# A new hand-written engine order for a cross-attention and PReLU kernel, with weight loads issued at other places and wider filler products

## The chip, the cores and the metric

The kernel runs on one core of one Trainium2 chip. The metric is device time in microseconds (us) of one execution, the median over runs. The engines are TensorE (PE in the profile; its weight loads are PEld), VectorE (DVE), ScalarE (ACT), GpSimd (POOL) and SyncE (SP). The first four compute; SP here only issues DMA transfers, and POOL and ACT issue some too.

## The reference

There are 8 batches of 8 heads. `x` is 512 tokens of 64 numbers per head, `state` 32 states of 64 numbers per head. Tokens read states and states read tokens, and all 544 rows of a batch then go through a two-layer network of widths 512, 2048, 512 with a PReLU between.

```python
scores = scale * np.matmul(x, state.transpose(0, 1, 3, 2))
a = softmax(scores)                       # over 32 states
xread = np.matmul(a, state)
scores2 = scale * np.matmul(state, x.transpose(0, 1, 3, 2))
a2 = softmax(scores2)                     # over 512 tokens
sread = np.matmul(a2, x)
x = np.concatenate([xread, sread], axis=2)   # heads side by side: (8 * 544, 512)
h = x @ w_in
g = np.maximum(h, 0.0) + alpha * np.minimum(h, 0.0)
out = g @ w_out
```

## The kernel before

**What is computed, and how.** For the tokens, `xread @ w_in` is not formed from `xread`: the states of a batch are multiplied into `w_in` first (`m`, line 445), and the softmax weights are then multiplied into that (`h`, lines 478 and 499). So the first product of the network has the states as its depth. For the rows that belong to states, all 8 batches are collected in `XS` and go through `w_in` at the end (line 487). The weights are kept in SBUF: `w_in` in four parts by columns of the hidden layer (`wi.0` to `wi.3`), `w_out` in four parts by its rows (`wo.0` to `wo.3`). A part is 512 KB as float16. Hidden columns are numbered in 16 pieces of 128 (`jc`): `wi.f` and `wo.f` both hold pieces 4f to 4f+3.

**The order.** The program is run from the string `ORDER` (lines 17 to 102): a list of some thousand steps. Each step is a short name, a dot, and arguments; the loop at line 607 calls the function of that name (table at line 593). Every engine works through its own steps in the order of the list, and waits at a step until what that step needs is there. Semaphores are put in from the data dependencies. The names, by engine:

- POOL, loads: `lx0.g` (half g of the first batch's x, line 179), `lx.b` (x of batch b, line 162), `lst` (all states but the first batch's, line 192), `wi.f` (line 198), `wo.i` (line 204). `id` makes the identity matrix that transposes use.
- TensorE: `Z.k.n` (n filler products of zeros of 128 columns into PSUM bank k, lines 213 to 217), `stt` and `str` (states transposed), `xt.b.j.g.k` (a quarter of x of batch b transposed, line 281), `sc.b` or `sc.b.half` (the scores, line 295), `m.b.f` (states times part f of w_in, line 445), `F.b.jc.k` (the first product of piece jc, two instructions, line 478; of the rows of states if b is 8, four instructions, line 487), `f.b.jc.g` (one half of such a product, line 499), `S.b.q.j` (second product: token quarter q, pieces 2j and 2j+1, line 530), `rd.b` (states reading tokens, line 420), `R` (second product of the rows of states, line 578), `L` (second product of the last quarter in three column pieces, line 550).
- DVE and ACT, `.a` for ACT, `.v` for DVE, `.p` for POOL: `xo` (transposed x out of PSUM), `sto`, `sro` (transposed states out), `mo.b.f.e.g` (a half of m out, line 467), `N.b.jc` (ACT: the negative part of h, line 510), `G.b.jc` (DVE: PReLU from h and N, line 518), `O.b.q` (an output quarter out of PSUM and to DRAM, lines 568 and 571), `rdo` (line 431), `stc` (the first states cast, line 238), `oma` (DVE: one less alpha from a loaded alpha, four transposes and one operation, lines 251 and 252).
- The softmax over states of batch b, a chain over three engines: `sb` (DVE: scores transposed in blocks, line 328 or 330), `smax` (DVE, line 336), `ssh` (POOL: subtract, line 342), `sexp` (ACT, line 348), `ssum` (DVE: sum and reciprocal, lines 352 and 353), `snorm` (POOL: multiply, line 356), `wb` (DVE: transposed back, line 364). Batch 0 does it in two halves, `.0` and `.1`.
- The softmax over tokens: `tm` (DVE, line 376), `te` (ACT, line 387), `tsum` (DVE, line 397), `tn` (POOL, line 401), `tt` (SP: transposed by DMA, line 405). `xd.b` (SP) transposes x of a later batch by DMA (line 273).

**PSUM.** Six banks are named 0 to 5 by the number at the end of a step, and one two-bank tile ("two") is shared by the scores and by those `m` that name no banks. A step that takes a bank waits until the reader of the bank's last content is through: for a piece of h that is its `G`, for an output its `O`, for an m its `mo`, for the scores `sb`, `tm` and `te`.

**Around the change.** Before the zero fillers there is a memset of a tile of zeros (line 211). Fillers stand at the head, where TensorE has nothing else to do. The head's real work is: transposes of the first states and of x of batch 0, its scores, m of part 0 for batches 0 to 3, transposes of x of batch 1, and then the first products f and F of batch 0, for which each part of w_in has to have landed.

```python
    zero = consts.tile([128, 128], F16)
    nc.vector.memset(zero, 0.0)

    def zeros(k, n):
        t = single(k, f"z_{len(zs)}", [128, 128], F32)
        zs.append(t)
        for _ in range(n):
            nc.tensor.matmul(t, zero, zero, start=True, stop=True)
```

Of the kernel before, what the change touches and what calls it, by code (L numbers as in the profile page):

```python
# [28 lines left out]
S.0.0.2 N.0.9 G.0.6 S.0.1.2 smax.1 te.1.1 te.1.0 F.0.11.4 G.0.9 ssh.p.1 F.0.8.3 N.0.8 N.0.11 S.0.0.3  # L29
S.0.1.3 m.0.3 G.0.8 F.0.10.0 mo.0.3.a.0 N.0.10 sexp.1 S.0.2.3 mo.0.3.v.1 xd.2 G.0.11 G.0.10  # L30
S.0.3.0.3 m.1.3 S.0.3.1 mo.1.3.a.0 F.0.14.4 S.0.2.4 F.0.13.0 N.0.14 tt.0 ssum.1 S.0.0.4 S.0.1.4
S.0.0.5 S.0.3.2 G.0.14 F.0.12.4 N.0.13 G.0.13 F.0.15.0 snorm.p.1 N.0.12 N.0.15 mo.1.3.a.1 wb.1
S.0.3.3 S.0.1.5 S.0.3.4 G.0.12 S.0.2.5 G.0.15 S.0.3.5 F.1.2.4 S.0.2.6 N.1.2 F.1.0.0 tsum.1 S.0.2.7
N.1.0 S.0.1.6 S.0.1.7 G.1.2 O.0.2.a sc.2 m.2.1.4.5 S.0.0.6 O.0.1.a F.1.7.2 mo.2.1.a.0 mo.2.1.a.1
G.1.0 F.1.1.0 tm.2 sb.2 F.1.3.4 N.1.7 S.0.0.7 S.0.3.6 N.1.1 G.1.1 N.1.3 tn.1.0 O.0.0.a te.2.0
F.1.5.5 S.0.3.7 N.1.5 G.1.3 F.1.9.0 S.1.1.0.1 G.1.7 F.1.4.4 smax.2 O.0.3.a S.1.1.1 tn.1.1 G.1.5
rd.0.2 te.2.1 N.1.9 G.1.9 m.2.3 F.1.6.3 N.1.4 rdo.0.a F.1.12.5 N.1.6 lx.3 G.1.4 F.1.13.2 N.1.12
F.1.8.0 G.1.6 G.1.12 S.1.2.0.4 N.1.13 G.1.13 ssh.p.2 N.1.8 S.1.1.2 F.1.11.3 G.1.8 F.1.10.5 N.1.11
S.1.2.1 N.1.10 G.1.11 G.1.10 S.1.2.2 sexp.2 S.1.1.3 ssum.2 F.1.14.2 F.1.15.0 snorm.p.2 mo.2.3.a.0
S.1.1.4 mo.2.3.a.1 S.1.1.5 m.3.2 m.4.2.3.5 N.1.14 tt.1 tsum.2 N.1.15 G.1.14 mo.3.2.a.1 S.1.1.6  # L40
S.1.2.3 S.1.2.4 mo.3.2.a.0 mo.4.2.a.0 G.1.15 mo.4.2.a.1 S.1.2.5 S.1.1.7 xd.3 O.1.1.a m.3.1.2.0
m.2.2.3.5 sc.3 wb.2 tn.2.1 S.1.2.6 S.1.2.7 mo.3.1.a.1 F.2.15.1 S.1.0.0.0 mo.2.2.a.0 mo.3.1.a.0
O.1.2.a lx.4 mo.2.2.a.1 sb.3 N.2.15 S.1.0.1 tm.3 F.2.13.3 N.2.13 G.2.15 S.1.0.2 F.2.4.2 tn.2.0
F.2.2.4 G.2.13 smax.3 N.2.4 F.2.9.5 F.2.0.1 N.2.9 S.1.0.3 S.1.0.4 G.2.9 S.1.0.5 N.2.2 N.2.0 te.3.0
F.2.12.3 S.1.0.6 N.2.12 G.2.2 G.2.4 G.2.0 xd.4 F.2.7.5 G.2.12 S.1.3.0.4 ssh.p.3 sexp.3 N.2.7 ssum.3
S.1.0.7 te.3.1 F.2.3.2 S.1.3.1 F.2.1.1 N.2.3 S.1.3.2 N.2.1 F.2.8.3 G.2.3 S.1.3.3 G.2.1 S.1.3.4
S.1.3.5 N.2.8 S.1.3.6 G.2.7 F.2.6.2 O.1.0.a N.2.6 m.3.3.1.0 G.2.8 sc.4 rd.1.5 snorm.p.3 F.2.5.3
G.2.6 mo.3.3.a.0 F.2.14.1 rdo.1.a wb.3 N.2.5 tsum.3 S.2.1.0.2 F.2.11.5 mo.3.3.a.1 G.2.5 S.1.3.7
N.2.14 F.2.10.0 F.3.4.3 G.2.14 N.2.11 S.2.1.1 F.3.1.1 lx.5 O.1.3.v N.3.4 S.2.1.2 N.2.10 G.2.11 tt.2
S.2.0.0.4 S.2.1.3 S.2.0.1 G.2.10 F.3.14.5 F.3.9.0 S.2.1.4 tn.3.1 N.3.1 N.3.9 G.3.1 S.2.1.5 S.2.0.2  # L50
G.3.4 tn.3.0 N.3.14 tm.4 F.3.3.1 F.3.8.3 G.3.14 N.3.8 G.3.9 S.2.1.6 S.2.1.7 S.2.0.3 S.2.3.0.5 N.3.3
xd.5 O.2.1.a tt.3 sb.4 G.3.8 smax.4 F.3.6.0 F.3.2.2 te.4.0 S.2.3.1 S.2.3.2 N.3.6 N.3.2 F.3.13.3
S.2.0.4 te.4.1 ssh.p.4 N.3.13 G.3.3 G.3.6 S.2.0.5 F.3.7.1 G.3.2 S.2.0.6 N.3.7 S.2.0.7 sexp.4 G.3.13
G.3.7 S.2.3.3 S.2.3.4 S.2.3.5 m.6.0 O.2.0.v m.5.1.0.2 mo.6.0.a.1 mo.5.1.a.1 rd.3.3 mo.6.0.v.0
rdo.3.a mo.5.1.v.0 rd.2.1 m.4.1.4.2 ssum.4 sc.5 m.4.3.0.3 rdo.2.a S.2.3.6 mo.4.1.a.1 mo.4.1.a.0 tm.5
tsum.4 snorm.p.4 F.3.5.1 mo.4.3.a.0 mo.4.3.a.1 F.3.0.2 F.3.10.4 N.3.0 S.2.3.7 O.2.3.a S.2.2.0.0
S.2.2.1 F.3.11.3 G.3.0 wb.4 S.2.2.2 S.3.3.0.5 F.3.15.2 S.3.3.1 N.3.5 lx.6 G.3.5 te.5.0 te.5.1 N.3.10
N.3.15 S.2.2.3 F.3.12.1 S.2.2.4 N.3.11 S.3.3.2 lx.7 N.3.12 G.3.10 G.3.15 F.4.6.4 N.4.6 tn.4.0
F.4.5.2 G.3.11 F.4.3.3 N.4.5 S.2.2.5 G.3.12 G.4.5 S.3.3.3 F.4.4.1 S.3.3.4 F.4.7.2 N.4.4 S.3.3.5
S.2.2.6 N.4.3 sb.5 N.4.7 S.3.3.6 S.2.2.7 G.4.4 G.4.7 S.3.3.7 F.4.1.1 F.4.0.2 xd.6 O.2.2.a S.3.1.0.0  # L60
O.3.3.a S.3.1.1 F.4.9.5 N.4.1 smax.5 G.4.6 N.4.0 S.3.0.0.4 tn.4.1 S.3.0.1 G.4.1 G.4.0 F.4.8.1
S.3.1.2 tsum.5 N.4.9 ssh.p.5 G.4.3 sexp.5 N.4.8 G.4.9 F.4.11.2 F.4.2.3 N.4.2 S.3.0.2 ssum.5 S.3.0.3
S.3.0.4 tt.4 N.4.11 S.3.1.3 G.4.8 S.3.1.4 S.3.1.5 G.4.2 S.3.1.6 snorm.p.5 m.5.0.5.1 G.4.11 sc.6
m.5.3.3.2 xd.7 wb.5 mo.5.0.a.1 sb.6 S.3.1.7 mo.5.3.a.0 mo.5.0.a.0 F.4.13.1 N.4.13 S.3.0.5 mo.5.3.a.1
S.3.2.0.3 tm.6 S.3.0.6 te.6.0 F.4.10.5 F.5.3.2 smax.6 S.3.2.1 N.4.10 N.5.3 S.3.2.2 S.3.2.3 S.3.0.7
S.3.2.4 S.3.2.5 S.3.2.6 ssh.p.6 G.4.13 O.3.1.a tn.5.0 F.4.14.1 te.6.1 O.3.0.v S.3.2.7 G.4.10 G.5.3
N.4.14 F.4.12.0 G.4.14 O.3.2.a sexp.6 tn.5.1 S.4.1.0.4 m.6.3 m.7.2.5.2 m.5.2.3.1 mo.6.3.v.0 S.4.1.1
mo.5.2.v.0 mo.7.2.a.0 S.4.1.2 mo.5.2.a.1 F.5.15.5 mo.6.3.v.1 mo.7.2.a.1 tt.5 S.4.1.3 N.5.15 G.5.15
F.4.15.3 F.5.12.1 S.4.1.4 F.5.5.2 N.4.12 F.5.13.5 S.4.1.5 N.5.12 N.4.15 G.4.12 tsum.6 G.4.15
S.4.0.0.0 S.4.1.6 S.4.1.7 N.5.5 S.4.0.1 S.4.2.0.3 O.4.1.v G.5.5 S.4.0.2 F.5.10.4 N.5.13 F.5.1.2  # L70
S.4.2.1 G.5.12 F.5.0.1 N.5.10 S.4.0.3 S.4.2.2 S.4.0.4 G.5.13 tn.6.1 N.5.0 G.5.10 N.5.1 G.5.1
m.6.1.5.4 m.7.0 mo.6.1.a.1 mo.6.1.a.0 S.4.0.5 mo.7.0.v.0 S.4.0.6 F.5.2.2 N.5.2 S.4.0.7 mo.7.0.v.1
G.5.0 O.4.0.a rd.4.4 rd.5.5 G.5.2 m.7.3.1.0 rdo.4.a m.6.2.2.4 sc.7 rdo.5.a ssum.6 mo.7.3.a.0
mo.6.2.a.0 snorm.p.6 tn.6.0 S.4.3.0.5 S.4.3.1 mo.7.3.v.1 F.5.11.1 S.4.3.2 sb.7 S.4.3.3 N.5.11 G.5.11
F.5.6.2 F.5.9.0 S.4.2.3 S.4.2.4 F.5.7.1 S.4.3.4 mo.6.2.a.1 F.5.8.4 smax.7 S.4.3.5 S.4.3.6 wb.6
S.4.3.7 S.4.2.5 N.5.9 N.5.8 N.5.7 G.5.9 O.4.3.a G.5.8 F.5.4.0 N.5.4 tt.6 S.5.0.0.4 S.5.2.0.5 S.4.2.6
G.5.7 G.5.4 F.5.14.1 S.5.2.1 tm.7 S.5.0.1 N.5.6 S.4.2.7 F.6.3.0 N.5.14 G.5.6 S.5.2.2 S.5.0.2 te.7.1
F.6.15.2 N.6.3 G.6.3 S.5.2.3 N.6.15 S.5.2.4 S.5.0.3 G.6.15 ssh.p.7 S.5.2.5 F.6.7.0 S.5.1.0.2 N.6.7
S.5.0.4 G.5.14 O.4.2.v S.5.1.1 F.6.6.1 G.6.7 F.6.8.3 te.7.0 S.5.1.2 N.6.6 S.5.1.3 sexp.7 F.6.1.0
tsum.7 N.6.8 N.6.1 G.6.6 S.5.2.6 F.6.0.1 S.5.0.5 tn.7.1 tn.7.0 S.5.0.6 G.6.8 S.5.2.7 F.6.10.3 tt.7  # L80
N.6.0 S.5.1.4 G.6.1 S.5.1.5 S.5.1.6 S.5.1.7 F.6.14.0 N.6.10 O.5.1.a ssum.7 G.6.10 S.5.0.7 F.6.5.3
snorm.p.7 F.6.2.2 N.6.14 N.6.5 G.6.0 S.5.3.0.1 O.5.0.v G.6.14 m.7.1 G.6.5 rd.7.4 rd.6.0 rdo.7.v
N.6.2 O.5.2.a F.6.13.3 S.5.3.1 mo.7.1.v.0 rdo.6.a S.5.3.2 S.5.3.3 mo.7.1.v.1 F.6.9.5 F.8.4.4 N.6.9
G.6.2 S.5.3.4 wb.7 F.6.12.0 G.6.9 F.6.4.2 N.6.13 N.6.12 S.5.3.5 G.6.12 N.6.4 S.5.3.6 S.5.3.7
S.6.0.0.5 S.6.0.1 N.8.4 F.6.11.0 G.6.13 G.6.4 F.8.10.3 N.6.11 S.6.0.2 N.8.10 O.5.3.v G.8.4 S.6.1.0.2
F.7.0.1 S.6.0.3 F.7.7.4 N.7.0 S.6.1.1 G.6.11 S.6.0.4 N.7.7 S.6.0.5 G.7.0 S.6.1.2 F.8.14.0 S.6.1.3
S.6.1.4 G.8.10 S.6.0.6 N.8.14 F.7.3.1 S.6.0.7 G.7.7 S.6.1.5 F.8.3.3 F.7.6.4 G.8.14 N.7.3 F.8.2.0
O.6.0.v G.7.3 F.7.2.5 F.8.9.1 S.6.1.6 N.8.3 G.8.3 S.6.2.0.3 N.8.2 N.7.2 S.6.2.1 G.8.2 S.6.2.2 N.7.6
# [17 lines left out]
def kernel(  # L106
# [106 lines left out]
    def zeros(k, n):  # L213
        t = single(k, f"z_{len(zs)}", [128, 128], F32)
        zs.append(t)
        for _ in range(n):
            nc.tensor.matmul(t, zero, zero, start=True, stop=True)  # L217
# [422 lines left out]
```

## Time and profile before

| | |
|---|---|
| median of 3 runs | 218.81 us (218.28 to 219.42) |
| the profiled execution's own time | 219.05 us |
| its span, first to last instruction | 217.3 us |
| granted TensorE clock over the span | 1.00 |
| TensorE busy 0 to 5, 5 to 10, 10 to 15 us | 3.73, 4.53, 3.47 us |
| TensorE, DVE, ACT busy 20 to 25 us | 4.92, 5.00, 4.70 us |
| TensorE, DVE, ACT busy 100 to 120 us | 20.00, 18.62, 13.74 us |
| second product (L530), 496 instructions | 125.3 us busy, 379 ns each |
| first product (L478), 250 instructions | 68.3 us busy, 379 ns each |
| fillers (L217), 82 instructions | 7.5 us busy, 262 ns each |
| PReLU (L518), 128 full instructions | 89.9 us busy, 738 ns each |
| negative part (L510), 144 instructions | 76.9 us busy, 577 ns each |

Instructions of one engine overlap: a product of 512 columns lasts 379 ns, but the next starts 0.216 us after it. So a busy engine's rate is read from the starts of instructions that follow each other without a wait, not from the mean duration. Of the execution's 219.05 us, 1.75 lie around the span.

### The profile page before, as it was taken

What the parts mean: (1) busy time and instruction counts of PE and PEld (TensorE: products, weight loads), DVE (VectorE), ACT (ScalarE), POOL (GpSimd) and SP (SyncE); (2) the same over time, 40 slices, a digit from 0 to 9 for tenths busy, and PEclk for the clock granted to TensorE, in tenths of its full rate; (3) what the DMA queues carried; (4) which work ended last, traced back from release to release, by engine and by line L of the source; (5) the groups of instructions that cost most, each with busy time, mean ns of one, the idle gap of its engine ahead of it and who ended that gap; (6) DMA issues with size and microseconds to landing.
All of it is one profiled execution on the core that took longest, in us unless ns stands there. A gap on an engine that the chain in (4) does not pass through costs nothing.

```text
span 217.3 us, 4317 instructions
## 1 busy us (share of the span) xinstructions
PE 210.2 (97%) x1698; PEld 104.0 (48%) x1698; DVE 166.5 (77%) x255; ACT 137.6 (63%) x271; POOL 71.1 (33%) x58
## 2 busy tenths in 40 slices
...
GB/s 88 173 198 208 195 195 176 139 203 136 54 139 147 53 227 111 51 99 193 236 52 100 97 50 51 0 100 48 50 149 9 40 51 48 48 37 11 51 97 145
DMA packets 39716, 23.12 MB, mean 106 GB/s; under 512 B 22144, under 2 KB 35984, under 8 KB 39696
## 3 DMA queue, kind: packets, MB, share of 16 engines
...
q8 instruction: 13, 0.21, 0.4%
q14 instruction: 7, 0.06, 0.1%
...
## 4 chain that ended last, share of the span: by engine, by line
PE 87%; DMA 8%; POOL 2%; issue 1%; DVE 1%; ACT 0%; POOLq 0%
PE o L530 48%; PE h L478 24%; DMA w_in_sb<-in_moe_w_in_dram 5%; PE m_ps L445 4%; PE h L487 3%; PE o L578 3%; DMA xT<-xg 3%; PE o L550 2%; PE sr_ps L420 2%; PE sc L295 1%; DVE m L467 1%; POOL xg L179 1%; POOL xg L162 0%; PE h L499 0%; POOL w_in_sb L198 0%
## 5 line engine op out<-in xcount | busy, mean ns | idle before, releaser
L530 PE MATMUL o<-w_out_sb,gt 128*128 128x512 f16 x496 | 125.3, 379 | 0.0
L510 ACT ACTIVATE neg<-h 128x512 f32<-128x512 f32 (+1 forms) x144 | 76.9, 577 | 46.9 <-PE h L478 37.4
L518 DVE SCALAR_TENSOR_TENSOR gt<-neg,oma_sb,h 128x512 f16<-128x512 f32 x128 | 89.9, 738 | 15.8 <-ACT neg L510 14.7
L530 PEld LDWEIGHTS <-gt 128*128 128x128 f16 x496 | 47.3, 98 | 55.4 <-issue 3.4
L478 PE MATMUL h<-aT,m 128*128 128x512 f16 x250 | 68.3, 379 | 0.0
L478 PEld LDWEIGHTS <-m 128*128 128x128 f16 x250 | 24.1, 98 | 28.4 <-issue 0.6
L401 POOL TENSOR_SCALAR e<-e,r 128x512 f16<-128x512 f16 x16 | 25.0, 1568 | 21.1 <-DVE r L397 17.5
L467 ACT CAST m<-m_ps 128x512 f16<-128x512 f32 x50 | 27.0, 603 | 5.0 <-PE m_ps L445 4.6
L356 POOL TENSOR_TENSOR an<-ts,r 128x1024 f16<-128x1024 f32 (+1 forms) x9 | 15.5, 1720 | 33.9 <-DVE r L353 14.8
L342 POOL TENSOR_TENSOR ts<-ts,mx 128x1024 f32<-128x1024 f32 (+1 forms) x9 | 15.5, 1721 | 28.5 <-DVE mx L336 28.5
L568 ACT COPY osb<-o 128x512 f32<-128x512 f32 x22 | 12.9, 591 | 14.9 <-PE o L530 14.9
L445 PE MATMUL m_ps<-w_in_sb,stT 64*32 64x512 f16 x256 | 11.3, 383 | 0.9 <-DMA w_in_sb<-in_moe_w_in_dram 0.7
L387 ACT ACTIVATE e<-sc,nb 128x512 f16<-128x512 f32 x16 | 11.1, 700 | 1.1 <-DVE nb L379 1.1
L364 DVE STREAM_TRANSPOSE aT<-an 128x1024 f16<-128x1024 f16 (+1 forms) x9 | 10.1, 1120 | 1.8 <-POOL an L356 1.8
L518 DVE SCALAR_TENSOR_TENSOR gs<-neg,oma_sb,h 128x256 f16<-128x256 f32 x16 | 7.5, 478 | 4.5 <-ACT neg L510 4.5
L467 DVE CAST m<-m_ps 128x512 f16<-128x512 f32 x14 | 9.1, 679 | 2.1 <-ACT m L467 1.6
L352 DVE TENSOR_REDUCE r<-ts 128x32 f32<-128x1024 f32 (+1 forms) x9 | 9.9, 1095 | 0.0
L336 DVE TENSOR_REDUCE mx<-ts 128x32 f32<-128x1024 f32 (+1 forms) x9 | 9.8, 1092 | 0.0
L376 DVE TENSOR_REDUCE nb<-sc 128x2 f32<-128x1024 f32 x8 | 9.6, 1204 | 0.3 <-PE sc L295 0.3
L487 PE MATMUL h<-XS,w_in_sb 128*128 128x256 f16 x64 | 9.4, 273 | 0.0
L588 DVE COPY osr<-o 128x512 f32<-128x512 f32 x1 | 0.7, 691 | 11.3 <-PE o L578 11.3
L217 PE MATMUL z<-zero 128*128 128x128 f16 x82 | 7.5, 262 | 1.4 <-DVE zero L211 1.1
...
## 6 DMA issues: line engine op xcount, KB each, us to landing
...
```

Of the source, the lines that this page charges most:

```text
L342: engine(e).tensor_tensor(ts, ts, over_blocks(cols(live["mx", b], j, S // N)), ALU.subtract)
L356: engine(e).tensor_tensor(blocks(cols(live["an", b], j, S)), blocks(cols(live["ts", b], j, S)), over_blocks(cols(live["r1", b], j, S // N) ...
L387: nc.scalar.activation(live["e2", b][:, g, :, :], live["sc", b][:, :, :, g, :].rearrange("p r j s -> p (r j) s"), EXP, bias=live["nb", b][ ...
L401: nc.gpsimd.tensor_scalar_mul(e2, e2, live["r2", b][:, g : g + 1])
L445: nc.tensor.matmul(t[N * k : N * (k + 1), :], st_head(b, h)[64 * r : 64 * r + 64, :], w_in_sb[64 * r : 64 * r + 64, c, 512 * f : 512 * (f ...
L467: copier(e)(m_tile(b)[:, f, g, :], live["mp", b, f][g])
L478: nc.tensor.matmul(h.rearrange("p (r j s) -> p r j s", r=2, j=2), ms[b][:, f, g, 128 * j : 128 * (j + 1)], weights(b, g), start=(g == 0), ...
L487: nc.tensor.matmul(h, w_in_sb[:, c, 128 * jc : 128 * (jc + 1)], XS[:, c].rearrange("p q n b -> p (q n b)"), start=(c == 0), stop=(c == n_c ...
L510: nc.scalar.activation(neg, h, RELU, bias=0.0, scale=-1.0)
L518: nc.vector.scalar_tensor_tensor(gt, negs.pop((b, jc)), oma_sb[:, jc : jc + 1], h, ALU.mult, ALU.add)
L530: nc.tensor.matmul(outs[b, q], gts[b, jc][:, 128 * q : 128 * (q + 1)], w_out_sb[:, jc, :], start=(jc == 0), stop=(jc == n_jc - 1),)
L568: copier(e)(osb, t)
```

## The change

Four things are changed.

1. The tile of zeros is 512 columns wide, and `Z.k.n` now makes n times 128 columns in as few instructions as possible, up to 512 columns each. The fillers' numbers are changed in the list.
2. In the head, the loads are issued earlier in POOL's sequence: wo.0 and wi.2 directly behind wi.1, ahead of the first batch's `ssh`; wo.2, lx.2 and wo.3 directly behind both `tn` of batch 0. The sequence of the loads among themselves stays as it is.
3. Steps of the head change place or engine: `oma` comes behind the first two copies of x, `sto` goes from ACT to DVE, the x copies and the copies of m change engines and order, `m.0.1` uses the two-bank tile.
4. The list behind that, up to the sixth batch, is another sequence of the same steps, with other banks, and with some copies on another engine (`snorm` of batch 4 and `ssh` of batch 7 on DVE, for instance). In the last part, from the middle of the first products of batch 7 on, the sequence is the same but for the numbers of the banks.

```diff
 ORDER = """
-stc lx0.0 lx0.1 oma id Z.1.20 stt.0 Z.2.18 xt.0.0.0.1 sto.a xt.0.1.0.2 xo.0.0.0.v lst xo.0.1.0.v
-Z.0.6 sc.0.0 xt.0.1.1.3 xt.0.0.1.4 sb.0.0 xo.0.0.1.v smax.0.0 xo.0.1.1.a str.0.5 sc.0.1 str.1.0 wi.0
-sro.0.a lx.1 wi.1 ssh.p.0.0 sb.0.1 Z.1.3 sc.0 Z.5.7 m.0.0.1.2 sro.1.a sexp.0.0 smax.0.1 m.3.0.3.4
-ssh.p.0.1 tm.0 mo.0.0.a.1 sexp.0.1 ssum.0.0 m.1.0.5.0 ssum.0.1 te.0.1 te.0.0 mo.1.0.v.1 wo.0
-mo.1.0.a.0 snorm.p.0.0 mo.3.0.a.1 Z.2.28 xt.1.1.1.2 xt.1.1.0.5 mo.0.0.a.0 snorm.p.0.1 wb.0.0
-mo.3.0.a.0 m.2.0 xt.1.0.1.0 xo.1.1.0.v xt.1.0.0.4 f.0.0.0.1 f.0.1.0.5 wi.2 mo.2.0.a.0 wb.0.1
-mo.2.0.a.1 f.0.1.1 xo.1.0.0.v N.0.1 m.0.1.3.4 f.0.0.1 mo.0.1.a.1 m.1.1 xo.1.1.1.v N.0.0 xo.1.0.1.v
-mo.0.1.v.0 f.0.2.0.2 F.0.3.0 f.0.2.1 F.0.4.3 mo.1.1.v.0 mo.1.1.a.1 F.0.7.4 G.0.1 N.0.2 G.0.0 wo.1
-F.0.5.5 N.0.3 G.0.2 wi.3 m.4.0 N.0.4 S.0.0.0.1 N.0.5 G.0.3 tsum.0 S.0.1.0.2 N.0.7 mo.4.0.a.1 G.0.4
-S.0.0.1 S.0.1.1 G.0.5 mo.4.0.a.0 tn.0.1 m.0.2.0.3 sc.1 G.0.7 S.0.2.0.5 mo.0.2.a.0 tm.1 m.1.2.0.4
-wo.2 tn.0.0 mo.0.2.a.1 mo.1.2.a.0 S.0.2.1 lx.2 wo.3 sb.1 F.0.6.3 F.0.9.0 mo.1.2.a.1 N.0.6 S.0.2.2
...
+lx0.0 lx0.1 stc id Z.1.24 stt.0 lst wi.0 sto.v Z.2.13 xt.0.1.0.1 xt.0.0.0.2 xo.0.1.0.v xo.0.0.0.v
+Z.0.6 sc.0.0 xt.0.0.1.3 oma xo.0.0.1.a lx.1 wi.1 wo.0 sb.0.0 xt.0.1.1.4 xo.0.1.1.v str.0.5 sc.0.1
+sro.0.a smax.0.0 sb.0.1 str.1.0 smax.0.1 wi.2 sro.1.a ssh.p.0.0 Z.1.3 sc.0 ssh.p.0.1 Z.5.3 m.0.0.1.2
+tm.0 sexp.0.0 m.1.0.3.4 mo.0.0.a.0 ssum.0.0 sexp.0.1 m.2.0.5.0 ssum.0.1 mo.1.0.v.1 te.0.0 Z.1.22
+xt.1.1.1.1 mo.2.0.a.1 mo.2.0.a.0 xt.1.0.1.0 snorm.p.0.0 xt.1.0.0.5 wb.0.0 mo.0.0.a.1 snorm.p.0.1
+mo.1.0.a.0 xt.1.1.0.4 xo.1.0.1.a m.3.0.2.3 f.0.0.0.0 xo.1.1.1.v wb.0.1 te.0.1 f.0.1.0.1 wo.1 f.0.1.1
+mo.3.0.v.0 mo.3.0.a.1 wi.3 xo.1.0.0.v m.0.1 f.0.0.1 xo.1.1.0.v mo.0.1.v.1 f.0.2.0.2 m.1.1.3.5 N.0.1
+mo.0.1.a.0 F.0.3.4 G.0.1 f.0.2.1 tsum.0 N.0.0 mo.1.1.a.0 N.0.2 N.0.3 F.0.5.1 m.4.0 tn.0.1 F.0.4.3
+G.0.0 mo.1.1.v.1 tn.0.0 F.0.6.0 G.0.2 N.0.5 mo.4.0.a.0 wo.2 G.0.3 lx.2 N.0.4 S.0.0.0.5 S.0.1.0.2
+G.0.5 mo.4.0.a.1 S.0.1.1 sc.1 m.0.2.4.1 N.0.6 mo.0.2.a.0 mo.0.2.a.1 G.0.4 S.0.0.1 S.0.2.0.3 G.0.6
+m.1.2.4.0 S.0.2.1 mo.1.2.a.0 mo.1.2.a.1 sb.1 tm.1 F.0.7.1 F.0.9.4 S.0.1.2 N.0.7 N.0.9 F.0.11.0 G.0.7
+S.0.0.2 S.0.2.2 smax.1 te.1.0 te.1.1 F.0.10.1 S.0.0.3 S.0.2.3 N.0.11 wo.3 G.0.9 m.0.3 N.0.10
+mo.0.3.a.0 F.0.8.4 G.0.11 ssh.p.1 S.0.1.3 N.0.8 mo.0.3.v.1 tsum.1 sexp.1 S.0.3.0.0 S.0.3.1 m.1.3
+tn.1.0 G.0.10 F.0.15.1 G.0.8 F.0.12.4 mo.1.3.a.1 S.0.0.4 xd.2 S.0.2.4 S.0.2.5 N.0.12 S.0.3.2 N.0.15
+ssum.1 G.0.12 F.0.13.4 S.0.0.5 snorm.p.1 G.0.15 N.0.13 S.0.1.4 S.0.1.5 F.0.14.1 G.0.13 S.0.3.3
...
+lx.4 mo.3.2.v.1 S.1.2.5 rdo.1.a S.1.1.7 S.1.2.6 tn.2.0 mo.3.2.a.0 mo.4.2.a.1 O.1.1.a m.3.1.2.3 sc.3
...
+N.3.14 mo.6.0.a.1 mo.6.0.a.0 mo.5.1.a.1 S.2.0.4 ssum.4 S.2.0.5 S.2.0.6 mo.5.1.a.0 G.3.14 S.2.0.7
+tsum.4 m.4.1.0.1 snorm.v.4 O.2.0.a mo.4.1.a.0 sc.5 m.4.3.3.2 rd.2.5 mo.4.1.a.1 rd.3.4 S.2.2.0.0
...
-    zero = consts.tile([128, 128], F16)
+    zero = consts.tile([128, 512], F16)
     nc.vector.memset(zero, 0.0)
 
     def zeros(k, n):
-        t = single(k, f"z_{len(zs)}", [128, 128], F32)
+        t = single(k, f"z_{len(zs)}", [128, 512], F32)
         zs.append(t)
-        for _ in range(n):
-            nc.tensor.matmul(t, zero, zero, start=True, stop=True)
+        while n:
+            w = 128 * min(n, 4)
+            nc.tensor.matmul(t[:, :w], zero[:, :128], zero[:, :w], start=True, stop=True)
+            n -= w // 128
```

139 lines of the change are left out of this document (66 added, 73 removed).

## The prediction

> **What bounds the kernel now.** I read the page first, then the chain of waits in order of time, then the timeline of TensorE around the chain's first long piece, then the landings of the loads.
>
> ```profile
> PE 210.2 (97%) x1698; PEld 104.0 (48%) x1698; DVE 166.5 (77%) x255; ACT 137.6 (63%) x271; POOL 71.1 (33%) x58
> ...
> PE 87%; DMA 8%; POOL 2%; issue 1%; DVE 1%; ACT 0%; POOLq 0%
> ```
>
> And of the chain in order of time (start, length, what):
>
> ```profile
> 5.68 11.78 DMA w_in_sb<-in_moe_w_in_dram
> 18.90 0.43 PE h L478 x2
> ...
> 64.59 5.99 DMA xT<-xg
> ```
>
> The reader is to see one long wait at the head, the load wi.1 (second quarter of w_in), which POOL issues at 5.68 and which lands at 5.68 + 11.78 = 17.46 us, and after it almost only TensorE. The stage table says the same: from 17.5 us on TensorE is idle for some 0.4 us in all. So the end is "wi.1 has landed" plus the products that come after it plus the store of the last piece. The timeline of TensorE shows what stands before that point:
>
> ```profile
> 11.28 0.84 PE L445 MATMUL m_ps<-w_in_sb,stT 64*32 64x512 f16 x24 [0.37 <-DMA w_in_sb<-in_moe_w_in_dram]
> 12.39 1.72 PE L217 MATMUL z<-zero 128*128 128x128 f16 x28 [0.28 <-ACT m L467]
> 15.00 0.62 PE L281 MATMUL xT_ps<-ident,xg 128*128 128x128 f16 x8 [0.88 <-DMA xg<-in_x_dram]
> 15.55 0.41 PE L445 MATMUL m_ps<-w_in_sb,stT 64*32 64x512 f16 x8
> 15.89 0.62 PE L281 MATMUL xT_ps<-ident,xg 128*128 128x128 f16 x8
> 16.35 0.81 PE L499 MATMUL h<-aT,m 128*128 128x512 f16 x3
> 17.50 0.41 PE L445 MATMUL m_ps<-w_in_sb,stT 64*32 64x512 f16 x8 [0.34 <-DMA w_in_sb<-in_moe_w_in_dram]
> ```
>
> The three loads wi.0, lx.1, wi.1 each end a hole (11.28, 15.00, 17.50). The products in front of the last hole are issued until 17.0 (16.35 and three times 0.216), so the softmax chain of the first batch has about 0.5 us to spare. The loads themselves, by line and issue:
>
> ```profile
> L198 POOL DMA_DIRECT2D w_in_sb<-in_moe_w_in_dram x1: 774/774/774, 5.7 to 5.7; - x1
> DMA to landing us min/median/max: 11.8/11.8/11.8
> ...
> L204 POOL DMA_DIRECT2D w_out_sb<-in_moe_w_out_dram x1: 787/787/787, 11.7 to 11.7; - x1
> DMA to landing us min/median/max: 8.3/8.3/8.3
> ...
> L198 POOL DMA_DIRECT2D w_in_sb<-in_moe_w_in_dram x1: 806/806/806, 15.0 to 15.0; - x1
> DMA to landing us min/median/max: 7.5/7.5/7.5
> ```
>
> Issue plus time to landing: wi.1 17.5, wo.0 20.0, wi.2 22.6; with the other answers wi.0 11.2, lx.1 15.0, wo.1 25.2, wi.3 27.7, wo.2 30.2. From lx.1 on one load of 512 KB lands every 2.5 to 2.6 us, whether it was issued 12 us or 7 us before. POOL's queue is never empty up to wi.3: it works first in, first out, at its full rate.
>
> **The change, part by part.** All sums are against the profiled execution: span 217.3, its time 219.05, so 1.75 lies around the span. The median of the runs is 218.81; I carry the difference over to that.
>
> *Loads of w_out and w_in moved forward.* The order within POOL's queue stays: lx0.0, lx0.1, lst, wi.0, lx.1, wi.1, wo.0, wi.2, wo.1, wi.3, wo.2, lx.2, wo.3. What changes is the issue: wo.0 and wi.2 directly behind wi.1, at about 6.45 and 7.2 in place of 11.74 and 15.05. POOL's two issues (0.79 + 0.81) end by 8.05, before the first ssh, which waits for DVE until 9.39 in before. As the queue is full, no landing up to wi.3 moves: gain 0, and wi.1 still lands at 17.46. Both later loads that POOL issues behind tn.0.1 and tn.0.0 come some 1 to 2 us earlier; nothing waits for them now. So 0. The Trainium skill (DMA: Bandwidth & Descriptors, Queues, rings and completion order) says that each DMA engine consumes a ring's descriptors in ring order; the landings 2.5 us apart agree, and by that rule too the sum for this part is 0.
>
> *The zeros.* In columns of 128 the fillers go from 20 + 18 + 6 + 3 + 7 + 28 = 82 to 24 + 13 + 6 + 3 + 3 + 22 = 71, up to four columns' worth in one instruction. The two fillers ahead of the first transposes of x go from 38 to 37 units at about 0.107 us each (20 took 2.31 us), so the transposes start at 5.6 to 5.9 instead of 5.84. The memset of the zeros is four times as wide: 0.11 us before, so at least 0.11 and at most 0.44; I take 0.3, near the upper end. A 512-wide product of zeros has no row; I take four narrow ones (bounds: the 0.216 us of a warm L478 and 4 x 0.107 cold). All this lies ahead of lx.1 at 15.0, so 0. The last filler, 22 units at 0.056 us (28 took 1.72 less a drain of 0.2), ends at 13.65 in place of 14.0, so the hole before lx.1 grows from 0.88 to about 1.35 us.
>
> *The softmax chain of batch 0.* oma (1.06 us on DVE) moves from 2.97, where DVE idles, to between the first copies of x and sb.0.0. It lands on a wait of 0.42 us for the scores, and the copies come some 0.2 us earlier, so sb.0.0 starts at 8.0 and not 7.69, and the chain behind it is 0.3 us late: snorm.0.1 ends at 15.4 and not 15.09. wb.0.1 waited behind a copy of x's batch 1 until 16.00 anyhow, so it still ends at 16.7: cost 0. Without that cover it would be 0.3, of which the 0.5 us ahead of wi.1 hide all. Bounds: from 0 to the whole 1.06, which would cost 1.06 - 0.5 = 0.5 us.
>
> *A new wait at m.0.1.* It now takes the two-bank tile, so it also waits for te.0.1, the last reader of the scores. On ACT that stands behind xo.1.0.1 (a copy of 0.6 us, possible after its transposes at 15.65): 15.65 + 0.6 + 0.77 = 17.0 at the latest sum. wi.1 lands at 17.46, so 0.45 us are left; queued behind te.0.1 are mo.3.0.1 (0.6) and N.0.1, hence G.0.1, then F.0.5, which wants G.0.1's bank. I get G.0.1's end at 19.35 and F.0.5's turn at 19.38. Cost 0, with 0 to spare.
>
> *After m.0.1.* The same products are left, in another sequence. Full-width products follow each other every 0.432 us; a group of small ones (m, sc, rd) costs 0.09 at its entry and 0.115 at its exit (0.525 in place of 0.432, 0.341 in place of 0.226). I count 17 entries and 18 exits after m.0.1 in the old order, 18 and 19 in the new: +0.2 us. By the same steps the old order needs 194.8 us from m.0.1 to the end of the last product's turn; it took 196.5. So **1.7 us of small waits** is all that a new order can win. Four places make 1.1 of it: 0.27 at sc.1 (22.94), 0.37 and 0.12 around sc.4 (70.03), 0.32 before m.4.3 (89.55):
>
> ```profile
> 70.03 0.41 PE L445 MATMUL m_ps<-w_in_sb,stT 64*32 64x512 f16 x8
> 70.62 0.41 PE L295 MATMUL sc<-xT,stT 64*32 64x256 f16 x16 [0.18 <-DMA xT<-xg]
> ```
>
> The sc.4 one is the transposing DMA at 64.59 of the chain. Its load, lx.4, stands behind tn.2.1 in the old POOL order and is issued at 57.69; in the new one it goes ahead of both tn, at about 55, so the transposed x is there 2 us before sc.4: gain 0.4. Before m.4.3 the old order has no products between m.5.1 and the two rd; the new one has four S there (1.7 us), enough for the copies: gain 0.3. sc.1 now comes before m.0.2: gain 0.27. Against it I count 0.1 at S.0.1.1, which wants G.0.3 (21.4 to 22.1 by DVE's steps of 0.66) at 22.0, and for the rest of the new order, which has no row, 0 to 2 us: it has two reuses of a bank after 2.16 and 2.39 us where the old one's shortest of that width are 2.24 and 2.27, so I take a value near the low end, 0.25 more than the old small waits.
>
> **Sum:** 0 + 0 + 0 + 0 + 0.2 - 0.4 - 0.3 - 0.25 + 0.1 + 0.25 = -0.4 us. Span 216.9, time **218.4**.
>
> **Rivals.**
>
> *All small waits go.* Then -1.7 + 0.2 = -1.5, time 217.3. For it: three of the four large ones have a visible cause that the new order removes. Against: waits of 0.1 for a bank or a copy come with any order in which DVE is 92% busy, as it is here from 20 to 100 us. 12%.
>
> *The clock closes in the longer hole (slower).* Place: 13.65 to 15.0. In before the zeros took 0.107 us each up to about 6.3 and 0.056 to 0.061 later, so the clock rose some 5.3 us after the first product; holes of 0.37, 0.28 and 0.88 did not lower it again. If 1.35 us does, what stands between 15.0 and 17.0 takes 2 us longer, so m.0.1 starts at some 19.3 (+1.8), and the remaining 1 us until the clock is back costs 0.5: +2.3, time 220.7. It decides between 0.88 and 1.35 us of idleness. 7%. The Trainium skill (TensorE: Matmul & The Clock Gate, Part 1: The HAM clock gate) puts the idle window at about 3.4 us; by that the hole is too short and the time stays 218.4. No run here shows the threshold.
>
> *DVE falls behind the new order.* Between tm.3 and G.3.6 the new order gives DVE up to 5.2 us more than TensorE does in the same stretch, by the steps of its rows; the old one's worst such excess is 3.8. If the 1.4 us between them come out as waits: 218.4 + 1.4 = 219.8, and with a second such place (F.0.12 to F.0.13 behind ssum.1) 220.3. Against: going through that stretch with DVE's steps I find every bank free 0.5 us before its turn. 15%.
>
> *The early issues do harm.* Six unfinished loads (lst, wi.0, lx.1, wi.1, wo.0, wi.2) would stand in the queue at 8 us; in before five do at most (at 5.7 and at 17). If its second extra issue had to wait until wi.0 has landed (11.25), ssh.0.0 would start at 12.05 and not 9.7, wb.0.1 would end at 18.7, and m.0.1 follow at 19.0: +1.5, time 219.9. Or, if the loads shared the rate in place of queueing, wi.1 would come with wi.2: 5.1 us later, 223.5. The regular landings speak against that. 6% and 2%.
>
> **How the numbers follow.** The forecast holds 58%. About 0.5% (1.1 us) is what a measurement of this kernel can tell from no change. Faster by more takes the first rival and a lucky forecast: 0.14. Slower by more: the gate 0.07, half of DVE 0.08, the early issues 0.06: 0.21. The rest, 0.65, is within. The range leaves out a part of the first rival below (217.4) and the gate and the shared rate above: 217.4 to 220.3. The forecast's own range is 217.7 to 219.5.
>
> **What would show it.** wo.0 and wi.2 issued before 8.5, and wi.1 still landing at 17.4 to 17.6, with m.0.1 directly behind it; a hole of 1.2 to 1.5 before 15.0; no wait at sc.4. If m.0.1 starts later than 17.6, the new wait on te.0.1, the chain or the clock was mispriced; if wi.1 lands earlier or later than that, my reading of the queue is wrong, and with it the whole forecast; if m.0.1 starts at 17.5 and the time is off by over 1 us, it is the order behind it.

## The result, and the profile after

The changed kernel takes 220.21 us (median of 7 runs, 220.12 to 221.09) where the kernel before took 219.03 (7 runs beside them, 218.28 to 219.42). The medians lie 1.18 us apart; the ratio given with the runs is 1.0081, with a 95% interval of 1.0064 to 1.0098: slower by 0.8%. Beside the later experiments before had medians of 218.47 to 218.68. The forecast was 218.4, slightly faster or no change.

The profiled execution took 220.13 us, its span is 218.4 (before 217.3). Line numbers of the changed kernel are those of before plus 2 behind the function `zeros`. First the page, busy times and the chain of waits by engine:

```profile
PE 210.2 (96%) x1636; PEld 98.8 (45%) x1636; DVE 168.2 (77%) x259; ACT 136.6 (63%) x269; POOL 68.0 (31%) x56
...
PE 81%; DVE 7%; ACT 5%; DMA 3%; issue 1%; POOL 1%; POOLq 0%
```

Before, TensorE held 87% of the chain, DMA 8% and DVE and ACT together 1%. Now DVE and ACT hold 12%: somewhere behind the head the end is set by them. The head itself, in TensorE's timeline:

```profile
11.65 0.84 PE L447 MATMUL m_ps<-w_in_sb,stT 64*32 64x512 f16 x24 [1.17 <-DMA w_in_sb<-in_moe_w_in_dram]
12.73 1.35 PE L218 MATMUL z<-zero 128*128 128x512 f16 x6 [0.24 <-ACT m L469]
14.36 1.15 PE L283 MATMUL xT_ps<-ident,xg 128*128 128x128 f16 x16 [0.27 <-DMA xg<-in_x_dram]
15.44 0.83 PE L447 MATMUL m_ps<-w_in_sb,stT 64*32 64x512 f16 x8
16.36 0.81 PE L501 MATMUL h<-aT,m 128*128 128x512 f16 x3
17.10 0.41 PE L447 MATMUL m_ps<-w_in_sb,stT 64*32 64x512 f16 x8
```

m.0.1 starts at 17.10 (17.50 before), directly behind the three f. The loads that were issued earlier, by line and issue:

```profile
L198 POOL DMA_DIRECT2D w_in_sb<-in_moe_w_in_dram x1: 774/774/774, 5.7 to 5.7; - x1
DMA to landing us min/median/max: 11.4/11.4/11.4
...
L204 POOL DMA_DIRECT2D w_out_sb<-in_moe_w_out_dram x1: 770/770/770, 6.4 to 6.4; - x1
DMA to landing us min/median/max: 13.2/13.2/13.2
...
L198 POOL DMA_DIRECT2D w_in_sb<-in_moe_w_in_dram x1: 777/777/777, 7.2 to 7.2; - x1
DMA to landing us min/median/max: 15.0/15.0/15.0
```

wo.0 is issued 5.3 us earlier and lands at 19.6 (20.0 before), wi.2 is issued 7.9 us earlier and lands at 22.2 (22.6 before); wi.1 lands at 17.1. So TensorE is 0.4 us earlier behind the head, and yet the last product ends at 215.34 us and not at 214.28. To find where, I took each step of TensorE behind m.0.1, and subtracted from the time to the next step's start the turn that the prediction uses (0.432 us for a full pair, 0.226 for an m or sc, 0.093 and 0.115 for entry and exit of a group of small products). What is left over is a wait:

| behind m.0.1, us | before | after |
|---|---|---|
| turns, by count | 194.92 | 195.17 |
| waits in all | 1.70 | 2.91 |
| of these at sc.1 | 0.27 | 0.43 |
| at S.0.1 | 0 | 0.22 |
| F.0.15 to F.0.12, at 31.7 us | - | 0.23 |
| 49 to 54 us: F.1.12, F.1.11, F.1.15 | - | 0.86 |
| m.2.2 to S.1.2.7, at 59 us | - | 0.41 |
| sc.4 and behind it | 0.48 | 0 |
| ahead of m.4.3 | 0.32 | 0 |
| S.4.1.1 to F.4.15, at 118 us | - | 0.25 |

-0.40 for the start, +0.25 of turns and +1.21 of waits make the +1.06 us at the last product. The largest wait is at 49 to 54 us. Its origin is in SP's timeline of the changed kernel (L573 is an output's store, L407 `tt`):

```profile
40.51 2.13 SPq L573 DMA_DIRECT2D out_dram<-osb  x2
42.69 1.30 SPq L407 DMA_TRANSPOSE e2T<-e  x1
44.04 0.89 SPq L573 DMA_DIRECT2D out_dram<-osb  x1
44.97 1.28 SPq L407 DMA_TRANSPOSE e2T<-e  x1
46.36 0.89 SPq L573 DMA_DIRECT2D out_dram<-osb  x1
```

The first L407 is tt.1, the second tt.0: in the new list tt.1 stands behind two outputs of batch 0, and tt.0 behind tt.1 and three outputs. SP works in order, so it can't issue tt.1 before the two outputs exist, though what tt.1 reads was ready at 37.4 us (the end of the last `tn` of batch 1 on POOL). In the kernel before tt.0 stood ahead of all outputs, and tt.1 behind them (its SP timeline):

```profile
36.40 1.30 SPq L405 DMA_TRANSPOSE e2T<-e  x1
40.34 5.78 SPq L571 DMA_DIRECT2D out_dram<-osb  x4
46.23 1.30 SPq L405 DMA_TRANSPOSE e2T<-e  x1
```

The two `tt` of the changed kernel by line 407, the one issued at 42.69 first:

```profile
L407 SPq DMA_TRANSPOSE e2T<-e x1: 1302/1302/1302, 42.7 to 42.7; - x1
...
who waited for it (us, times):
  ACT e L389: 1.4, 1
...
DMA to landing us min/median/max: 5.3/5.3/5.3
...
L407 SPq DMA_TRANSPOSE e2T<-e x1: 1281/1281/1281, 45.0 to 45.0; - x1
...
DMA to landing us min/median/max: 4.3/4.3/4.3
```

So ACT waited for tt.1, which landed at 48.0; tt.0 landed at 49.3, and nothing waited for it. The tile `e2` of the exponentials has two buffers. In these lists `te` of batch 2 takes over the one that is given back first in the list: here batch 1's, because tt.1 now stands ahead of tt.0, and it may be written only when tt.1 has landed. Three engines wait in turn. ACT, DVE and TensorE of the changed kernel:

```profile
48.06 0.69 ACT L389 ACTIVATE e<-sc,nb 128x512 f16<-128x512 f32 x1 [1.39 <-DMA e2T<-e]
...
48.74 2.05 ACT L512 ACTIVATE neg<-h 128x512 f32<-128x512 f32 x4
...
49.36 0.75 DVE L520 SCALAR_TENSOR_TENSOR gt<-neg,oma_sb,h 128x512 f16<-128x512 f32 x1 [0.78 <-ACT neg L512]
...
50.16 0.59 PE L480 MATMUL h<-aT,m 128*128 128x512 f16 x2 [0.35 <-DVE gt L520]
```

ACT stands for 1.39 us at te.2.1; N.1.13 and three more stand behind it on ACT; G.1.13 on DVE waits 0.78 for that; and F.1.12, which takes the bank that G.1.13 reads, waits on TensorE. In the kernel before, nothing waited for a `tt`: there `te` of batch 2 took batch 0's buffer, and tt.0 had landed at 39.8, four us ahead of it.

The trace has a landing reported in 16 parts. Of tt.1's, fifteen are there at 46.44, ahead of ACT's coming to te.2.1 at 46.67, and the last only at 47.98. So the wait takes both: tt.1 behind the stores, and one late part. In all five profiles of kernels with the new list throughout (this one and four of the experiments) this part is 1.5 to 1.6 us late; why, no run shows.

### The profile page after: what moved, and what is told of

It is laid out like the page before. It is cut to its first block, busy times and chain, and to the rows that moved or that the text cites. A ratio compares the mean times of both kernels' runs of the same rounds, so it can differ in the third digit from the quotient of the medians.

```text
span 218.4 us, 4192 instructions
## 1 busy us (share of the span) xinstructions
PE 210.2 (96%) x1636; PEld 98.8 (45%) x1636; DVE 168.2 (77%) x259; ACT 136.6 (63%) x269; POOL 68.0 (31%) x56
## 4 chain that ended last, share of the span: by engine, by line
PE 81%; DVE 7%; ACT 5%; DMA 3%; issue 1%; POOL 1%; POOLq 0%
PE o L532 45%; PE h L480 21%; DVE gt L520 4%; DMA w_in_sb<-in_moe_w_in_dram 3%; PE m_ps L447 3%; PE h L489 3%; PE o L580 3%; ACT m L469 3%; PE sr_ps L422 2%; ACT neg L512 2%; PE o L552 2%; PE sc L297 1%; DVE m L469 1%; DVE ts L330 1%; POOL xg L179 1%
## 5 line engine op out<-in xcount | busy, mean ns | idle before, releaser
L403 POOL TENSOR_SCALAR e<-e,r 128x512 f16<-128x512 f16 x16 | 25.7, 1611 | 27.4 <-DVE r L399 9.6
L344 POOL TENSOR_TENSOR ts<-ts,mx 128x1024 f32<-128x1024 f32 (+1 forms) x8 | 13.6, 1696 | 32.4 <-DVE mx L338 32.4
L358 POOL TENSOR_TENSOR an<-ts,r 128x1024 f16<-128x1024 f32 (+1 forms) x8 | 13.6, 1698 | 29.5 <-DVE r L355 22.9
L447 PE MATMUL m_ps<-w_in_sb,stT 64*32 64x512 f16 x256 | 12.1, 382 | 1.2 <-DMA w_in_sb<-in_moe_w_in_dram 1.2
L469 DVE CAST m<-m_ps 128x512 f16<-128x512 f32 x15 | 10.0, 677 | 2.1 <-PE m_ps L447 1.3
L489 PE MATMUL h<-XS,w_in_sb 128*128 128x256 f16 x64 | 8.9, 273 | 0.0
L330 DVE STREAM_TRANSPOSE ts<-sc 128x1024 f32<-128x1024 f32 x7 | 8.7, 1243 | 0.3 <-PE sc L297 0.3
```

What stands on the lines that cost most here:

```text
L344: engine(e).tensor_tensor(ts, ts, over_blocks(cols(live["mx", b], j, S // N)), ALU.subtract)
L358: engine(e).tensor_tensor(blocks(cols(live["an", b], j, S)), blocks(cols(live["ts", b], j, S)), over_blocks(cols(live["r1", b], j, S // N) ...
L403: nc.gpsimd.tensor_scalar_mul(e2, e2, live["r2", b][:, g : g + 1])
L447: nc.tensor.matmul(t[N * k : N * (k + 1), :], st_head(b, h)[64 * r : 64 * r + 64, :], w_in_sb[64 * r : 64 * r + 64, c, 512 * f : 512 * (f ...
L469: copier(e)(m_tile(b)[:, f, g, :], live["mp", b, f][g])
L489: nc.tensor.matmul(h, w_in_sb[:, c, 128 * jc : 128 * (jc + 1)], XS[:, c].rearrange("p q n b -> p (q n b)"), start=(c == 0), stop=(c == n_c ...
```

## The experiments

Each kernel differs from before or after by the edit shown. The two columns of sums are those of the table above, each from the kernel's own profiled execution; "m.0.1" is its start.

| kernel | median us | ratio to before (95%) | m.0.1 | turns | waits |
|---|---|---|---|---|---|
| new_head_old_rest | 218.75 | 1.0010 (0.9996-1.0023) | 17.57 | 194.92 | 1.32 |
| old_to_60_new_rest | 219.23 | 1.0028 (1.0015-1.0040) | 16.93 | 195.33 | 1.80 |
| new_tt0_first | 219.86 | 1.0053 (1.0034-1.0072) | 17.13 | 195.17 | 2.05 |
| new_three_moves | 219.37 | 1.0035 (1.0024-1.0046) | 17.82 | 195.17 | 1.97 |
| old_tt0_late | 226.39 | 1.0352 (1.0323-1.0381) | 17.42 | 194.92 | 8.96 |
| old_loads_early | 218.70 | 1.0008 (0.9994-1.0023) | 17.30 | 194.92 | 1.94 |
| old_head_new_rest | 221.71 | 1.0151 (1.0127-1.0176) | 18.30 | 195.17 | 2.05 |
| old_repaired | 218.24 | 0.9984 (0.9973-0.9996) | 17.19 | 195.13 | 0.82 |
| new_e2_three_buffers | 219.55 | 1.0043 (1.0031-1.0056) | 17.42 | 195.17 | 2.05 |
| new_e2_three_m_split | 219.66 | 1.0053 (1.0040-1.0066) | 17.07 | 195.17 | 2.05 |
| old_m_split | 218.36 | 1.0001 (0.9990-1.0012) | 17.20 | 194.92 | 1.32 |
| old_repaired_2 | 218.25 | 0.9985 (0.9974-0.9995) | 17.44 | 195.13 | 0.71 |

**Head or rest?** The new list up to its m.0.1 region (all steps that stand ahead of the old list's m.2.0), then the old list:

```diff
-<new list behind the head>
+<old list from m.2.0 on, without the steps already done, banks renamed>
```

> The new order's steps up to the first batch's m of part 0 (wide zeros, oma moved, wo.0 issued early), then the old order (banks renamed). Theory A (the loss is made of waits behind m.0.1 in the new order, the head is harmless): m.0.1 starts at 17.0 to 17.5, small waits after it 1.7 us as in before, time 0.0 to 0.4 us below before. Theory B (the head itself costs, by its zeros or its early loads): about 1 us above before.

It is as fast as before: 1.0010. So the wide zeros, the early wo.0, the moved `oma` and the changed copies cost nothing and win nothing; wi.2 and the loads behind it are issued as late as before here (wi.2 at 15.5 us). TensorE's timeline shows that the head now just reaches the limit itself: one product waits for the softmax weights from DVE (`aT`), and m.0.1 follows at 17.57 although the load of wi.1 was over by then.

```profile
17.27 0.38 PE L501 MATMUL h<-aT,m 128*128 128x512 f16 x1 [0.24 <-DVE aT L366]
```

**The early part or the late part of the rest?** The old list up to the steps that stand ahead of the new list's F.2.2 (about 60 us), then the new list.

```diff
-<new list up to F.2.2>
+<the same steps in the old list's order, banks renamed>
```

> The old order up to the middle of the first products of batch 2 (about 60 us), then the new order (banks renamed). Theory A (waits of the new order before 60 us): 0.5 us of small waits before 60 us, 0.5 us behind, 0.4 us more of product turns; 0.2 to 0.6 us below before. Theory C (the loss lies in the whole new order, also behind 60 us): 0.5 to 1 us above before.

0.3% slower than before, not faster: a miss. The sum explains it in part: the mixed list has 0.41 us more turns, as I had counted, and the seam cost 0.62 us of waits, which I had not. It still takes 0.5% less than the changed kernel, so most of the loss lies before 60 us.

**tt.0 moved, then three moves.**

```diff
-... O.0.0.a ... O.0.1.a ... tt.1 ... O.0.2.a ... F.1.13.5 tt.0 G.1.5
+... tt.0 O.0.0.a ... O.0.1.a ... tt.1 ... O.0.2.a ... F.1.13.5 G.1.5
```

> The new order with one step moved: the transposing DMA of batch 0's token weights (tt.0) goes ahead of the first output on SP's queue, and so ahead of tt.1. Theory A: the hole of 1.4 us on ACT at 46.7 and the waits of 0.5 and 0.1 us of TensorE at 49 and 50.6 go; 0.5 to 0.7 us below the new order, so 0.4 to 0.7 above before. Theory D (DVE is late there anyhow and the wait comes back some steps later): less than 0.2 us below the new order.

The three waits at 49 to 54 us are gone, 0.86 us of 2.91, and nothing came in their place; the time falls by some 0.3% of before, though the intervals of the two ratios overlap (1.0064 to 1.0098 and 1.0034 to 1.0072). With tt.0 first in the list, te.2.1 takes batch 0's buffer, which tt.0 had left at 38.9; tt.1 lands as late as ever, at 47.9, and nothing waits for it. In the second kernel two ACT copies were moved as well:

```diff
-N.0.4 S.0.0.0.5 S.0.1.0.2 G.0.5 mo.4.0.a.1
+mo.4.0.a.1 N.0.4 S.0.0.0.5 S.0.1.0.2 G.0.5
-mo.4.2.a.1 O.1.1.a
+O.1.1.a mo.4.2.a.1
```

> The new order with three steps moved: tt.0 as in the run with that alone; the second half of m.4.0's copy ahead of N.0.4 on ACT; the output copy O.1.1 ahead of a copy of m.4.2 on ACT. Theory A: the waits of 0.43 at 22 us, 0.5 and 0.1 at 49 to 51, 0.41 at 59 us go; 1.2 to 1.5 us below the new order, that is from 0.3 below to 0.1 above before. Theory D: the waits come back in other places; 0.5 us below the new order or less.

The wait at sc.1 went, but 0.31 us came back in three pieces at 23.4 to 24.9 us; the wait at m.2.2 did not go, it only stood one step earlier:

```profile
59.30 0.41 PE L447 MATMUL m_ps<-w_in_sb,stT 64*32 64x512 f16 x8 [0.24 <-ACT m L469]
```

So only a part of the theory held: the wait for the buffer can be taken out singly, the two others did not go by moving one copy.

**A wait for the buffer made in the old kernel.**

```diff
-N.0.14 tt.0 ssum.1 ... O.0.0.a te.2.0
+N.0.14 ssum.1 ... O.0.0.a tt.0 te.2.0
```

> The order of before with one move: the transposing DMA tt.0 stands behind the output copy O.0.0 (the third output of batch 0) in place of ahead of all outputs. Theory A (the place of tt.0 in SP's queue, behind outputs, cost the changed kernel its wait around 49 us): SP issues tt.0 at about 45.0 in place of 36.4, it lands some 3.1 us later (as in the changed kernel), so te.2.0 on ScalarE waits from 44.0 until 48.1; N.1.5 and G.1.5 come some 3 us late and TensorE waits 1.5 to 2.8 us between 47 and 55. Time 1.5 to 2.8 us above before. Rival (ScalarE and DVE have the slack, the wait of the changed kernel comes from its order of N and G): under 0.4 us.

One transposing DMA, issued 8 us later, costs 7.7 us, far more than I expected. Its timelines of SP, ACT and TensorE:

```profile
44.52 1.51 SPq L405 DMA_TRANSPOSE e2T<-e  x1
...
50.14 0.69 ACT L387 ACTIVATE e<-sc,nb 128x512 f16<-128x512 f32 x1 [6.02 <-DMA e2T<-e]
...
50.10 1.04 PE L420 MATMUL sr_ps<-e2T,xg 128*64 128x32 f16 x32 [3.77 <-DMA e2T<-e]
52.61 0.63 PE L445 MATMUL m_ps<-w_in_sb,stT 64*32 64x512 f16 x8 [1.47 <-ACT e L387]
```

And its table by stretch (bounds and length; busy time and instructions of PE, PEld, DVE, ACT, POOL; granted clock, DMA share, GB/s):

```profile
45.00:50.00 5.00, 1.33 (x7) 0.39 (x4) 1.55 (x2) 0.00 (x0) 1.90 (x1) 0.96 1.15 168
...
53.00:54.00 1.00, 1.00 (x10) 0.28 (x3) 0.92 (x2) 0.87 (x3) 0.00 (x0) 0.50 0.99 256
...
56.00:57.00 1.00, 1.00 (x5) 0.39 (x4) 0.89 (x2) 0.83 (x2) 0.00 (x0) 0.76 1.40 228
57.00:60.00 3.00, 3.00 (x16) 1.35 (x15) 2.43 (x4) 2.30 (x5) 0.00 (x0) 1.00 0.65 38
```

I had missed three things. In the old list rd.0, which reads what tt.0 writes, follows at once (46.2 us), so TensorE itself waited 3.8 us; in the new list rd.0 comes at 55 us. The transposition landed 5.5 us after its issue, not 3.1. And behind the hole the granted clock was 0.50 until about 56.5 us (a mean of 0.76 from 56 to 57), which made four full pairs last 0.4 us longer each. The direction is the theory's, the size is not a measure of the changed kernel's loss. And the transposition waited for is tt.0 here (in the old list tt.1 comes behind te.2.0), while in the changed kernel it was tt.1.

**The loads alone.**

```diff
-lx.1 wi.1 ssh.p.0.0 ... wo.0 ... wi.2
+lx.1 wi.1 wo.0 wi.2 ssh.p.0.0 ...
```

> The order of before with wo.0 and wi.2 directly behind wi.1 on POOL, and nothing else changed. Theory A (the prediction's step: the queue is full, no landing up to wi.3 moves): 0, within 0.3 us; wi.1's slowest engine ends between 16.5 and 17.5 as in all runs so far. Rival B (the early issues let wi.1 land earlier, and this is why the changed kernel starts m.0.1 at 17.10): m.0.1 at 17.1 or earlier and 0.4 us faster. Rival C (the loads share the rate): m.0.1 1 us later or more and as much slower.

1.0008 (0.9994 to 1.0023), as the prediction had it: issued 5 and 8 us earlier, the loads do nothing here.

**The other half of the cut.**

```diff
-<new head>
+<old head up to m.2.0, banks renamed>
```

> The head of before (all steps ahead of its m.2.0, with its zeros 128 columns wide and its late loads), then the changed kernel's order for all that is left. Theory A (the loss is in the order behind the head): as the changed kernel, 1.2 to 1.9 us above before, with its waits at sc.1 (0.43), at 49 to 53 us (0.85) and at m.2.2 (0.41). Rival (the loss needs the new head): under 0.8 us.

3 us slower, twice the expected loss. A part is the seam: m.2.0 in its old place takes a bank that the next transposes need (0.71 us of wait for ACT's copy), and m.0.1 starts at 18.30. The profiled execution was the fastest of six (220.49; the others 221.4 to 222.6), and in it the wait at 49 us is missing, since tt.1 landed 3.6 us after its issue and not 5.3, with no late part. What the other five lost is not in any trace, but the mean granted clock of four of them was 0.985 to 0.992, against 1.00 in the profiled one (and 0.983 to 0.985 in all runs of old_tt0_late): TensorE ran for a while at a lower clock there, so the 3 us are not a count of the new order's waits. It says that the loss needs no new head, and no more.

```profile
16.50 0.87 PE L281 MATMUL xT_ps<-ident,xg 128*128 128x128 f16 x8 [0.71 <-ACT m L467]
```

**A buffer instead of a move.**

```diff
-name=f"e2_{b}", tag="e2", bufs=2
+name=f"e2_{b}", tag="e2", bufs=3
```

> The changed kernel, order untouched, with three buffers in place of two for e2 (the exponentials that tt transposes). Then te.2 writes a buffer that tt.0 never read. Theory A (the wait at 49 to 53 us is te.2 waiting for tt.0, which stands behind outputs on SP): the 0.87 us of waits there go, as with tt.0 moved ahead: ratio to before 1.003 to 1.006. Rival (it is SP's order itself, the later tt.1 and xd.3, or the order of N and G, that costs): ratio stays at 1.008.

1.0043, and the waits are 2.05, the same as with tt.0 first. The order is untouched, so it is neither SP's sequence in itself nor the order of N and G: it is the buffer that te.2 takes over. I expected it to be the one that tt.0 holds; in the trace of the changed kernel it is tt.1's. Line 389 has no DMA among its waits any more (in the changed kernel it had "DMA e2T<-e: 1.4, 1"):

```profile
L389 ACT ACTIVATE e<-sc,nb x16: 680/704/781, 13.3 to 139.1; 128x512 f16<-128x512 f32 x16
its engine sat idle before it (us, times) until:
  issue: 0.4, 1
```

**Copies of one m on two engines.** In the changed kernel ACT's copy of one half of m.3.2 starts when DVE's copy of the other half ends, though both halves are ready:

```profile
57.19 0.69 DVE L469 CAST m<-m_ps 128x512 f16<-128x512 f32 x1
...
57.91 1.07 ACT L469 CAST m<-m_ps 128x512 f16<-128x512 f32 x2 [0.64 <-DVE m L469]
```

The edit keeps m in two tiles, one for each half:

```diff
-ms[b] = moe.tile([128, n_f, 2, 512], F16, name=f"m_{b}", tag="m", bufs=7)
+ms[b] = [moe.tile([128, n_f, 512], F16, name=f"m_{b}_{g}", tag=f"m{g}", bufs=7) for g in range(2)]
```

> The changed kernel with three buffers for e2 and, in addition, m kept in two tiles (one for each half g) in place of one tile with both halves; order untouched. Theory F (in the traces a copy of one half of m on VectorE starts only when ScalarE's copy of the other half has ended, and the other way round, because both write one tile; the new order gives halves to both engines at 30.2, 57.9 and 118.0 us and waits 0.59, 0.64 and 0.72 there): the TensorE waits at F.0.12 (0.23), m.2.2 (0.41) and F.4.15 (0.25) go or shrink, 0.5 to 0.9 us less than with three buffers alone: ratio 1.000 to 1.003. Rival (the copies wait for something else, such as the two-bank product): no difference from three buffers alone.

> The kernel before with m kept in two tiles, one for each half; order untouched. Theory F: VectorE's copies at 88.75 us no longer wait 1.16 us for ScalarE, so the 0.32 us ahead of m.4.3 goes, and perhaps 0.1 at m.1.3: 0.2 to 0.4 us below before, ratio 0.998 to 0.999. Rival: 0.

Nothing changes in either: 1.0053 beside 1.0043, and 1.0001. In the new kernel with two tiles the wait is still there to the hundredth (L471 is the same line, two lines further down):

```profile
57.02 1.07 ACT L471 CAST m<-m_ps 128x512 f16<-128x512 f32 x2 [0.64 <-DVE m L471]
```

That theory falls. All such places copy an m that stands in the two-bank PSUM tile. Where the halves stand in two banks of their own, the two engines copy at the same time, as with m.0.1 in the kernel before (its DVE, then its ACT):

```profile
17.95 0.69 DVE L467 CAST m<-m_ps 128x512 f16<-128x512 f32 x1 [0.28 <-PE m_ps L445]
...
18.01 0.59 ACT L467 CAST m<-m_ps 128x512 f16<-128x512 f32 x1 [0.22 <-PE m_ps L445]
```

In the changed kernel m.0.1 takes the two-bank tile, DVE copies its half from 17.58 to 18.27, and ACT waits 0.34 us for it and starts at 18.30. So the wait goes with that tile, as a semaphore that the program sets between the two copies; an edit that gives m.3.2 two banks of its own was not run.

**Repairs of the old kernel.**

```diff
-wb.2 tn.2.1 ... lx.4
+wb.2 lx.4 tn.2.1 ...
-N.0.5 ... N.0.7 mo.4.0.a.1 ... mo.4.0.a.0
+mo.4.0.a.1 N.0.5 ... mo.4.0.a.0 N.0.7
-S.2.3.3 S.2.3.4 S.2.3.5 m.6.0 O.2.0.v m.5.1.0.2 ... rd.3.3
+m.6.0 O.2.0.v m.5.1.0.2 ... S.2.3.3 S.2.3.4 S.2.3.5 rd.3.3
```

> The order of before with its own large waits attacked: lx.4 ahead of tn.2.1 on POOL; mo.4.0.a.1 ahead of N.0.5 and N.0.7 behind mo.4.0.a.0 on ScalarE (for sc.1); S.2.3.3 to S.2.3.5 between m.5.1 and rd.3 on TensorE (for m.4.3). If waits can be taken out singly: -0.27 at sc.1, -0.48 between m.5.1 and m.4.3 with +0.21 for one more group of small products, and 0 to -0.48 at sc.4 (in the kernel with the new head and the old rest that wait was 0.1 although lx.4 was issued at the same time): 0.5 to 1.0 us below before, with 0.7 to 1.0 us of waits left. Rival (a wait taken out comes back nearby, as at sc.1 in the kernel of three moves): within 0.3 us of before.

218.24 against 218.66: 0.9984 (0.9973 to 0.9996), the first kernel here that beats both, by 0.2% of before. Half of the waits are gone (0.82 left), for one more group of small products. m.0.1 started 0.3 us earlier in this execution, and that was given back at m.0.2, which waits for wi.2 in this execution:

```profile
22.96 0.41 PE L445 MATMUL m_ps<-w_in_sb,stT 64*32 64x512 f16 x8 [0.27 <-DMA w_in_sb<-in_moe_w_in_dram]
```

A second repair adds m in two tiles and one move:

```diff
-m.0.2.0.3 sc.1
+sc.1 m.0.2.0.3
```

> The repaired old order, with m in two tiles and sc.1 ahead of m.0.2 on TensorE. In the old order m.0.2 cannot start before 22.9 us, when wi.2 has landed, whatever m.0.1 does (22.93 to 22.96 in four profiles), and sc.1 stands behind it; put ahead, sc.1 runs in that wait. Theory: 0.2 to 0.3 us on top of the repaired old order's 0.42, together with what old_m_split gives elsewhere: ratio 0.9960 to 0.9980. Rival (sc.1 now waits for the copies of m.4.0, as in the changed kernel): no more than the repaired old order, 0.9984.

0.9985: no more than the repair before. sc.1 runs ahead of m.0.2 without a wait, but m.1.2 then waits 0.22 us for its bank.

## Why the prediction was wrong

**The bound and the loads: right.** wo.0 and wi.2 were issued before 8.5 and their landings moved by 0.4 us, as wi.1's did, and alone they are worth 1.0008. That wi.1 landed at 17.1 and not 17.46 is not the change: in the six profiles whose list is the old one up to m.0.1 and its loads, it started at 16.93 to 17.50. The sign that I had set, a landing at 17.4 to 17.6, was too narrow for that, and its miss says nothing against the reading of the queue.

**Zeros, `oma`, the wait for te.0.1: right, at 0.** The hole before lx.1 was 0.27 and not 1.35 us, because lx.1 landed at 14.3 and not at 15.0 and the fillers began later. The clock stayed at 1.00, so that rival did not come.

**The term of +0.2 for groups: right.** 195.17 against 194.92.

**The gains at sc.4 and m.4.3: there, but one was not the order's.** Both waits are gone, 0.48 and 0.32. In the old order, though, sc.4's wait was 0.72, 0.48 and 0.11 us in three profiles with the same step sequence around it (old_loads_early, before, old_m_split): it is the landing of one transposition, so a gain of 0.4 was read off a single execution. In the two with the longer waits the last of its 16 parts came 1.6 us behind the others (70.58 after 69.01 in before); in old_m_split no part was late. The reason that I gave did not come either: lx.4 was issued at 57.30, not at about 55, so only 0.4 us earlier than before.

**The gain at sc.1: wrong in sign.** I argued that sc.1 now stands ahead of m.0.2 and so needn't wait for it. It waits for ACT's copy of m.4.0, the tile it takes, and that copy stands behind N.0.5 and N.0.4: 0.43 in place of 0.27. In the kernel before it had waited for the same copy: the copy ended at 23.39 and sc.1 started at 23.44.

**The cost at S.0.1: 0.22 for 0.1.** I had named S.0.1.1, waiting for G.0.3. The wait is one step earlier, at S.0.1.0, for G.0.2, whose bank it takes and which ends at 21.43.

**The step that failed: "0.25 more than the old small waits" for the rest of the new order.** By the forecast some 0.9 us of waits were to be left there: 1.70 less the 0.27, 0.48 and 0.32 of the old places, and 0.25 more. It measured 2.26 (2.91 less 0.43 at sc.1 and 0.22 at S.0.1), and 0.86 of that is one thing: te.2.1 waiting for the buffer that tt.1 reads, behind two stores. I went through the new list for banks of PSUM and for DVE's load, with bounds of 0 to 2 us, and took a value near the low end by the shortest reuse of a bank. I didn't go through it for buffers in SBUF, nor for SP's queue, which the change also reorders. The rows that would have warned of it were there: tt.0 at 36.40 ahead of the stores at 40.34, and te.2 at 44.0, so a `te` of batch 2 can come a few us behind the stores. In the new list both `tt` stand behind stores; tt.1 is issued at 42.69 and has landed at 47.98, 1.3 us after ACT came to te.2.1. Two different edits that give te.2 a free buffer in time each take 0.3 to 0.4% off, of 0.8% in all. The rest is made of 0.25 us of turns and of waits of 0.2 to 0.4: sc.1, m.2.2 and F.4.15 wait for a copy on ACT, S.0.1 and F.0.12 for a PReLU on DVE (G.0.2 and G.0.8). Moving copies shifted them more than it removed them, and I have not shown each one's price by itself.

**The rivals.** "DVE falls behind" gave the nearest time (219.8 to 220.3) but for another place and engine: between tm.3 and G.3.6 there is no wait, and the wait that came has ACT standing still.
